# Reordering the passage between the frequency stage and the feed-forward stage of a long-convolution kernel

## The chip, the cores and the metric

The kernel runs on one core of a Trainium2 chip. The metric is the device time of one execution in microseconds (us). A core has a matmul engine (TensorE, PE), a vector engine (VectorE, DVE), a scalar engine (ScalarE, ACT), a general engine (GpSimd, POOL) and a queue engine that only issues transfers (SyncE, SP). Each engine works through its own instructions in order, and waits on semaphores for the others. Matmuls write into PSUM, which has eight banks; DVE and ACT read it, POOL cannot.

## The reference

The reference is a long convolution per channel, done as a product in the frequency domain, followed by a feed-forward layer whose hidden value is the maximum of three products.

```python
h_mlp = np.maximum(pos_emb @ w1, 0.0) @ w2
h_filt = h_mlp * np.exp(-0.01 * pos)[:, None]
u = x * v
Uf = np.fft.rfft(u, n=2 * S, axis=1)
Hf = np.fft.rfft(h_filt, n=2 * S, axis=0)
y = np.fft.irfft(Uf * Hf[None], n=2 * S, axis=1)[:, :S]
t = (x * y).reshape(B * S, D)
h = np.maximum(np.maximum(t @ w1_, t @ w2_), t @ w3_)
out = h @ w_out
```

B is 4, S is 12544, D is 128, and the hidden width is 768. Everything is in 32 bit floating point.

## The kernel before

**Stages.** The Fourier transform is split into factors that are matmuls with tables. For batch 0 a first stage takes 32 units of the product `x*v` to a spectrum `spec`. Then a loop over 46 steps goes through 45 groups of frequencies: second stage (`g_second`), filter spectrum (`s_second`, `s_filter`), product with the filter (`g_re`, `g_im`), and third stage (`g_third`), three steps later than the second. The third stage's result `zs` is copied out of PSUM by ACT and stored to a buffer in memory, `zd`. The feed-forward part then goes over tiles of four positions: it loads z for the tile (`t_load`), makes its even and odd sums (`t_sums`), does the last transform stage and multiplies by x (`t_last`, result `gt`), and then runs six up products (`up`) and six down products (`down`). Batches 1 to 3 are convolved beside the feed-forward part of the batch before them, with steps placed in slots; there `u_products` does the first stage of a unit in three parts: `top` (an ACT copy), `sums` and `fours` (four vector operations each).

**The passage.** Between the loop and the first tile the code does, in this order: unit 0 of batch 1 (`u_first(0)`), the third stage of group 43, unit 1, one fold, the third stage of the last group 44, and the other five folds with two turns between them. A fold multiplies two weight matrices so that the maximum can be done with two differences and a linear term `lin`: it transposes a slice of `w_sb[0]` on PE into a PSUM bank, ACT copies it out (`w1t`), and a later matmul adds into `pl`. `folding` holds the matmul back by two folds. Then the pools of this stage are closed, those of the next are opened in the same memory, and tile 0 and tile 1 are loaded. Units 2, 3 and 4 are done ahead of the first up product.

**Banks.** Third stages, unit 1's first bank and the folds' banks all come from one PSUM pool with three banks under one tag (`cps0`, tag `cv`). A tile takes a bank that has been given back, and a bank is given back when the last instruction that uses its tile is done. The two banks of the folds are used in turn until the last fold. Unit 1's first bank is read last by the first pair of `fours` (L484).

**Queues.** z stores and tables go out on SP, in program order. In the loop `g_third` issues the z store, and the table for a later third stage (`load_dir`) is asked for after it. The z of tile 0 is loaded on POOL's queue, all groups but the last; the last group's two rows go through a small buffer `ze`, stored on SP and ACT and loaded on SP. x for tiles 0 and 1 is loaded on POOL's queue ahead of z. In the feed-forward part an up product uses three PSUM banks in turn (`hps`): the first product is copied out by ACT, the second is taken by DVE in the maximum (L852).

Of the kernel before, what the change touches and what calls it, by code (L numbers as in the profile page):

```python
# [95 lines left out]
def kernel(  # L96
# [15 lines left out]
    nc = tc.nc  # L112
# [4 lines left out]
    NF = DFF // P  # L117
    NK = N1 // 2
# [529 lines left out]
                                    op=op)  # L648
        abs_[g] = ab

    def g_third(g):
        w, ab = ws.pop((g, 1)), abs_.pop(g)
        ps = state["cv"][1].tile([P, 512], FP32, tag="cv", name="ps3")
        for k in range(2):
            for q in range(2):
                halves_mm(ps[:, (2 * k + q) * D:(2 * k + q + 1) * D], w[:, k, q, :],
                          ab[:, k, q, :], k == 0 and q == 0, True)
        if g < NK - 2:
            zs = state["cv"][0].tile([P, 2, 256], FP32, tag="z", name="zs", bufs=2)
        else:  # L660
            zs = lwp.tile([P, 2, 256], FP32, tag="w1", name="zs")
        nc.scalar.copy(zs[:].rearrange("p k f -> p (k f)"), ps[:])
        if g == NK - 1:
            for c in range(2):
                (nc.scalar if c else nc.sync).dma_start(ze[c], zs[64 * c:64 * c + 2])
        nc.sync.dma_start(
            zd[0][2 * g:2 * g + 2].rearrange("k c t f -> (c t) k f"), zs[:])
# [106 lines left out]
    def x_load(b, i, eng):  # L774
        xT = hp.tile([D, 2, 4, NB], FP32, tag="xT", name="xT", bufs=2)
        for c in range(GC):
            eng.dma_start(xT[c * NG:(c + 1) * NG].rearrange("d i p n -> d (i p) n"),  # L777
                          x[:, 4 * i:4 * i + 8, c, b, :])
        xTs[b, i], xTs[b, i + 1] = xT[:, 0], xT[:, 1]

    def t_load(b, i):
        if b == i == 0:
            x_load(b, i, nc.gpsimd)
        zt = hp.tile([N1, 2, 512], FP32, tag="zt", name="zt", bufs=2)
        for c in range(2):
            if b == 0:
                n = NK if i else NK - 1
                (nc.sync if i else nc.gpsimd).dma_start(
                    zt[NK * c:NK * c + n],
                    zd[b].rearrange("(g a) c t f -> g a c t f", a=2)[  # L790
                        0:n, :, c, 2 * i:2 * i + 2, :].rearrange("g a t f -> g a (t f)"))
                if i == 0:
                    nc.sync.dma_start(
                        zt[NK * c + n:NK * c + NK].rearrange("o a (t f) -> o a t f", t=2),
                        ze[c:c + 1].rearrange("o t a f -> o a t f"))
                continue
            q, j = divmod(i, NT // 2)
            for a in range(2):
                nc.sync.dma_start(
                    zt[NK * c:NK * c + NK, a].rearrange("g (t f) -> g t f", t=2),  # L800
                    zd[b].rearrange("(g a) c t q f -> g a c t q f", a=2)[
                        :, a, c ^ (a & q), 2 * j:2 * j + 2, q, :])
        zts[b, i] = zt[:, 0], zt[:, 1]
        if i % 2 == 0 and (b or i > 2):
            x_load(b, i, nc.gpsimd if 0 < i < NT - 2 and b < B - 1 else nc.sync)

# [37 lines left out]
    def up(i, f, tag="hid", bufs=3):  # L844
        rhs = gs[i][:].rearrange("d p n -> d (p n)")
        h = (hidp if tag == "hid" else lp).tile([P, N], FP32, tag=tag, name="hid", bufs=bufs)
        pa = next(hbanks)
        halves_mm(pa[:, 0:N], w_sb[1][:, f * P:(f + 1) * P], rhs, True, True)
        nc.scalar.activation(h[:], pa[:, 0:N], Relu)  # L849
        pb = next(hbanks)  # L850
        halves_mm(pb[:, 0:N], w_sb[2][:, f * P:(f + 1) * P], rhs, True, True)
        nc.vector.tensor_tensor(out=h[:], in0=h[:], in1=pb[:, 0:N], op=ALU.max)  # L852
        return h
# [128 lines left out]
    def load_dir(g, a):  # L982
        w = lwp.tile([P, 2, 2, P], FP32, tag=f"w{a}", name="wt")
        nc.sync.dma_start(w[:].rearrange("p k r m -> p (k r m)"), wt_d[g, :, a, :])
        return w
# [73 lines left out]
    wf, wi = {}, {}  # L1059
# [30 lines left out]
    cps = pro.enter_context(tc.tile_pool(name="cps0", bufs=3, space=PSUM))  # L1090
# [75 lines left out]
    def folding(f):  # L1166
        folded.append(fold(f))
        if len(folded) > 2:
            folded.pop(0)()

    for s in range(NK + 1):
        if s < NK:
            ws[s, 0] = wf[s]
            s_second(s)
            g_second(s)
            wf.pop(s)
            if s + 3 < NK:
                wf[s + 3] = load_dir(s + 3, 0)
        if 1 <= s <= NK:
            g_swap(s - 1)  # L1180
            s_filter(s - 1)
        if s >= 3:
            ws[s - 3, 1] = wi.pop(s - 3)
            g_third(s - 3)
            if s < NK:
                wi[s] = load_dir(s, 1)
        ready = [g for g in {NK: (s - 2, s - 1)}.get(s, (s - 2,)) if 0 <= g and s <= NK]
        for g in {NK - 2: (s - 2, s - 1), NK - 1: (s - 1,), NK: (s - 1,)}.get(s, (s - 2,)):
            if 0 <= g and s <= NK:
                s_store(g)  # L1190
        for g in ready:
            g_re(g)
            g_im(g, 1 < s < NK - 2)
            if s == NK:
                g_unfold(g)
        if s < NK:
            s_sums(s)
            g_butterfly(s)
            for g in ready:
                g_unfold(g)  # L1200

        if s in muls:
            u_mul(muls[s])
        if s in turns:
            u_turn(turns[s])
        if s in loads:
            u_load(1, loads[s])

    def one_bank(pool, tag):
        return pool.tile([P, 512], FP32, tag=tag, name="ps1")[:]  # L1210
# [6 lines left out]
    pl = sps.tile([P, 512], FP32, tag="pl", name="pl")  # L1217
    u_first(1, (one_bank(cps, "cv"), hb), "x")
    fb = one_bank(cps, "cv")
    folds = iter((fb,))  # L1220
    folding(0)
    ws[NK - 1, 1] = wi.pop(NK - 1)
    g_third(NK - 1)
    folds = itertools.cycle((one_bank(cps, "cv"), fb))
    turn_banks = iter((g0, g1))
    state["turn"] = lambda: next(turn_banks)
    for f in range(1, NF):
        folding(f)
        if f in (2, 3):
            u_turn(f + 2)  # L1230
# [17 lines left out]
    cps = conv.enter_context(tc.tile_pool(name="cps", bufs=1, space=PSUM))  # L1248
# [15 lines left out]
    for n, (b, i) in enumerate(tiles[:LAST]):  # L1264
        if i == 0:
            plan, pairs_from = plans[b]
        if n == 0:
            t_load(*tiles[0])
            t_load(*tiles[1])
            nc.gpsimd.dma_start(sign_t[:], sign_d)  # L1270
            second_ = u_products(2, (next(hbanks), next(hbanks)))
            second_[0]()
            first_ = ops.tile([D, 512], FP32, tag="ops", name="ps1")
            spare = state["bank"]()
            third = u_products(3)
            fourth = u_products(4, (spare[:, 0:512], spare[:, 512:1024]), "xs")
            t_sums(tiles[0], nc.vector)
            third[0]()
            second_[1]()
            fourth[0]()  # L1280
            t_last(tiles[0], first_)
            second_[2]()
            for fn in fourth[1:]:
                fn()
        for f in range(NF):

            if i < NT - 2:
                if f == 0:
                    t_load(*tiles[n + 2])
            elif i == NT - 1 and f < 2 and n + 1 + f < len(tiles):  # L1290
                t_load(*tiles[n + 1 + f])
            turn_ = i == NT - 1
            if f == 3 and n == 0:
                x_load(b, 2, nc.gpsimd)
            if f == 4 and n + 1 == LAST:
                t_sums(tiles[n + 2], nc.vector)
            h = up((b, i), f)
            if n == 0 and f in (1, 2):
                third[f]()
            for a in range(2):  # L1300
                if f == plan[i][a]:
                    t_sums(tiles[n + 1],
                           nc.vector if turn_ or i * NF > pairs_from else nc.gpsimd, (a,))
            late.append(((b, i), f, h))
            if len(late) > 2:
                down(*late.pop(0))
            if f == plan[i][2]:
                t_last(tiles[n + 1])
            if f == 5 and n + 1 == LAST:
                t_last(tiles[n + 2])  # L1310
            run(besides.pop(n * NF + f, ()))
# [9 lines left out]
    cps = ctx.enter_context(tc.tile_pool(name="cps2", bufs=1, space=PSUM))  # L1321
# [18 lines left out]
    step, b = 0, B - 1  # L1340
    for i in range(0, NT, 2):
        h = {}
        X, Y = banks if i % 4 == 0 else banks[::-1]
        for j, (name, f) in enumerate(ORDER):
            n = int(name[1]) - 1
# [66 lines left out]
```

## Time and profile before

| what | value |
|---|---|
| median of three runs | 2205.84 us (2205.76 to 2206.69) |
| the profiled execution's own time | 2205.64 us |
| its span, first to last instruction | 2203.9 us |
| PE, DVE, ACT, POOL busy | 2186.5, 1533.7, 1211.4, 1183.3 us |
| frequency loop of batch 0 | about 110 to 268 us |
| passage | about 267 to 288 us |

A share of busy time is an average over stages with different limits. The passage is a hundredth of the span, so it is read in the timeline of the single engines and in stretches of a few us, and not in the page's groups. In the timeline a row gives the start, the duration from the first to the last of merged instructions, engine, line, operation, output and input, the count, and in brackets the idle time ahead of it and what ended it. "SPq" and "ACTq" are rows of a queue that issues transfers.

### The profile page before, as it was taken

The page shows a single profiled execution, that of the slowest core. Times are in us where ns is not written, and L with a number is a line of the kernel's source. Part 1 is how long each engine was busy: PE and PEld are TensorE (multiplying, and loading weights), DVE is VectorE, ACT ScalarE, POOL GpSimd, SP SyncE. Part 2 cuts the span into 40 slices and gives each one's busy share as a digit, 9 for nine tenths or more (in the row PEclk, how much of TensorE's full clock was granted, in tenths as well). Part 3 has the DMA queues.
Part 4 walks back from the last instruction along what each step waited for, and adds up shares of the span by engine and source line. Part 5 has one row for each costly group of instructions (what it writes and reads, how often), then busy time and mean ns, then how long its engine had stood idle before and what let it go on. Part 6 is the DMA issues. An engine that isn't in the chain of part 4 may idle for free.

```text
span 2203.9 us, 77207 instructions
## 1 busy us (share of the span) xinstructions
PE 2186.5 (99%) x31655; PEld 1258.5 (57%) x31655; DVE 1533.7 (70%) x3292; ACT 1211.4 (55%) x2223; POOL 1183.3 (54%) x1580
## 2 busy tenths in 40 slices
PE   9999999999999999999999999999999999999998
PEld 8988855555555555555555455555555545555565
DVE  5688966678888766668888766668878745454443
ACT  3699845466666555466666555456666522222222
POOL 1166568545544667535455566534545326666665
PEclk9999999999999999999999999999999999999999
DMA  8789999879999899789999899879999622222221
GB/s 200 184 262 318 302 181 206 170 196 247 248 245 246 209 189 178 155 193 243 245 245 251 212 193 175 171 172 244 242 251 241 179 75 59 65 71 69 59 59 24
DMA packets 491270, 411.62 MB, mean 187 GB/s; under 512 B 289379, under 2 KB 407901, under 8 KB 490917
## 3 DMA queue, kind: packets, MB, share of 16 engines
q1 hardware_dynamic: 443495, 274.33, 57.5%
q0 software_dynamic: 45936, 130.43, 20.9%
q8 instruction: 249, 4.08, 0.8%
q10 hardware_dynamic: 1486, 1.93, 0.4%
q14 instruction: 104, 0.85, 0.1%
HBM read 262.85 MB, written 84.68 MB: 158 GB/s over the span
## 4 chain that ended last, share of the span: by engine, by line
PE 93%; DVE 2%; POOL 2%; issue 1%; DMA 0%; ACT 0%; POOLq 0%; ACTq 0%; DVEq 0%
PE hps L169 46%; PE ops L169 20%; PE ops L913 6%; PE cps L169 4%; PE cps L549 3%; PE cps L451 3%; PE ps L178 3%; PE cps L559 3%; PE ps L169 2%; POOL xt L640 1%; PE last L169 1%; DVE ab L647 1%; PE ps L393 1%; DVE xs L639 1%; POOL specH L640 1%
## 5 line engine op out<-in xcount | busy, mean ns | idle before, releaser
L169 PE MATMUL hps<-gt,w_sb 128*64 128x392 f32 (+1 forms) x7672 | 1151.8, 494 | 1.8 <-DVE hid L852 1.0
L849 ACT ACTIVATE hid<-hps 128x392 f32<-128x392 f32 x768 | 382.4, 498 | 745.2 <-PE hps L169 726.9
L169 PEld LDWEIGHTS hps<-gt,w_sb 128*64 128x64 f32 (+1 forms) x7672 | 413.7, 126 | 454.5 <-issue 415.9
L852 DVE TENSOR_TENSOR hid<-hid,hps 128x392 f32<-128x392 f32 x768 | 428.5, 558 | 339.9 <-PE hps L169 321.4
L169 PE MATMUL ops<-hid,wo_sb 128*64 128x392 f32 x2304 | 476.8, 492 | 0.0
L601 POOL TENSOR_TENSOR cb<-cb,xs 128x512 f32<-128x512 f32 x135 | 178.2, 1320 | 358.3 <-DVE xs L598 349.8
L169 PEld LDWEIGHTS ops<-hid,wo_sb 128*64 128x64 f32 x2304 | 165.7, 137 | 213.5 <-issue 213.5
L574 DVE TENSOR_TENSOR cb<-cps,eo 128x512 f32<-128x512 f32 (+1 forms) x288 | 175.2, 650 | 78.0 <-ACT eo L571 76.9
L867 POOL DMA_DIRECT2D out_dram<-ot x96 | 77.1, 803 | 263.6 <-ACT ot L865 247.3
L589 ACT ACTIVATE xs<-cb 32x512 f32<-32x512 f32 x270 | 169.5, 628 | 21.9 <-DVE cb L574 13.1
L590 ACT COPY xs<-cb 32x512 f32<-32x512 f32 x270 | 166.3, 616 | 3.1
L605 DVE TENSOR_TENSOR xs<-cb 128x256 f32<-128x256 f32 x270 | 148.3, 598 | 7.3 <-POOL cb L601 7.3
L431 ACT COPY uT<-turned 113x512 uint16<-113x512 uint16 x180 | 125.9, 770 | 1.9 <-DMA turned<-planes 1.7
L388 POOL TENSOR_TENSOR ut<-ut 128x392 f32<-128x392 f32 x90 | 92.8, 1032 | 43.1 <-DMA ut<-in_vr_dram 42.9
L582 POOL DMA_DIRECT2D zd<-cb x135 | 93.8, 695 | 39.9 <-DVE cb L574 36.8
L169 PEld LDWEIGHTS cps<-f4p,even 90*64 90x64 f32 x1552 | 87.2, 138 | 35.9 <-issue 33.1
L777 POOL DMA_DIRECT2D xT<-in_x_dram x172 | 101.4, 605 | 4.6 <-DVE ab L647 3.1
L473 DVE TENSOR_TENSOR low<-high,cps 128x180 f32<-128x180 f32 x186 | 54.7, 336 | 68.9 <-ACT high L463 68.9
L938 POOL DMA_DIRECT2D out_dram<-o x120 | 72.6, 610 | 45.6 <-DVE o L931 44.5
L169 PE MATMUL cps<-f4p,zt 90*64 90x49 f32 x1552 | 95.9, 222 | 0.0
L415 POOL COPY planes<-ut 128x392 uint16<-128x392 uint16 x180 | 94.9, 561 | 0.0
L169 PE MATMUL cps<-f4p,even 90*64 90x49 f32 x1552 | 94.6, 220 | 0.0
(173 smaller groups left out, 3306.1 us busy)
## 6 DMA issues: line engine op xcount, KB each, us to landing
ht<-hd SPq DMA_DIRECT2D x264, 256.0 KB, 6.8
wt<-wq_const POOLq DMA_DIRECT2D x144, 256.0 KB, 5.6
zd<-cb POOLq DMA_DIRECT2D x135, 256.0 KB, 5.1
zt<-zd SPq DMA_DIRECT2D x384, 90.0 KB, 3.8
sq<-spec SPq DMA_DIRECT2D x528, 64.0 KB, 5.9
ut<-in_xr_dram SPq DMA_DIRECT2D x128, 196.0 KB, 4.0
ut<-in_vr_dram SPq DMA_DIRECT2D x128, 196.0 KB, 4.3
wt<-wt_const SPq DMA_DIRECT2D x90, 256.0 KB, 5.1
```

What stands on the lines that cost most here:

```text
L169: nc.tensor.matmul(out[h:h + w], lhsT[:, h:h + w], rhs, start=start, stop=stop, skip_group_check=True)
L415: nc.gpsimd.tensor_copy(w[:, h, :, :, 0:HB], a[:].bitcast(U16).rearrange("p s (m e h) -> p h s e m", e=2, h=2)[:, h])
L431: nc.scalar.copy(uts[u][0:HR, 8 * (u % 2):8 * (u % 2) + 8].rearrange("n s r t -> n (s r t)").bitcast(U16).rearrange("n (s r t h) -> n h s ...
L574: nc.vector.tensor_tensor(out=cb[:, a, lo:hi], in0=ps[:, lo:hi], in1=eo[:, lo:hi], op=op)
L589: nc.scalar.mul(xs[at:at + 32], xt[at + 32:at + 64], -1.0)
L590: nc.scalar.copy(xs[at + 32:at + 64], xt[at:at + 32])
L601: nc.gpsimd.tensor_tensor(out=xts[g], in0=xts[g], in1=xs[:], op=ALU.add)
L605: nc.vector.tensor_tensor(out=ab[:, q], in0=y[:, 0], in1=y[:, 1], op=(ALU.subtract, ALU.add)[q])
L777: eng.dma_start(xT[c * NG:(c + 1) * NG].rearrange("d i p n -> d (i p) n"), x[:, 4 * i:4 * i + 8, c, b, :])
L849: nc.scalar.activation(h[:], pa[:, 0:N], Relu)
L852: nc.vector.tensor_tensor(out=h[:], in0=h[:], in1=pb[:, 0:N], op=ALU.max)
L913: nc.tensor.matmul(ps[32 * q:32 * q + 32, 0:H2], w[:, m:m + 32], rhs[:, H2 * c:H2 * c + H2], start=start, stop=True, skip_group_check=True)
```

## The change

Four edits. (1) Two folds instead of one come ahead of the last third stage, and both banks of the folds are taken there. (2) In the loop the table for a later third stage is asked for inside `g_third`, after its matmuls and ahead of the copy and store of z. (3) The loads of z for tile 0 come ahead of those of x on POOL's queue. (4) Unit 4's `sums` and `fours` come behind the first and the second up product of tile 0, and no longer ahead of the first.

```diff
-    def g_third(g):
+    def g_third(g, then=None):
         w, ab = ws.pop((g, 1)), abs_.pop(g)
         ps = state["cv"][1].tile([P, 512], FP32, tag="cv", name="ps3")
...
                           ab[:, k, q, :], k == 0 and q == 0, True)
+        if then:
+            then()
         if g < NK - 2:
...
     def t_load(b, i):
-        if b == i == 0:
-            x_load(b, i, nc.gpsimd)
         zt = hp.tile([N1, 2, 512], FP32, tag="zt", name="zt", bufs=2)
...
         zts[b, i] = zt[:, 0], zt[:, 1]
+        if b == i == 0:
+            x_load(b, i, nc.gpsimd)
...
-            g_third(s - 3)
-            if s < NK:
-                wi[s] = load_dir(s, 1)
+            g_third(s - 3, (lambda: wi.update({s: load_dir(s, 1)})) if s < NK else None)
...
     fb = one_bank(cps, "cv")
-    folds = iter((fb,))
-    folding(0)
+    folds = itertools.cycle((fb, one_bank(cps, "cv")))
+    for f in range(2):
+        folding(f)
     ws[NK - 1, 1] = wi.pop(NK - 1)
     g_third(NK - 1)
-    folds = itertools.cycle((one_bank(cps, "cv"), fb))
     turn_banks = iter((g0, g1))
     state["turn"] = lambda: next(turn_banks)
-    for f in range(1, NF):
+    for f in range(2, NF):
         folding(f)
...
             t_last(tiles[0], first_)
             second_[2]()
-            for fn in fourth[1:]:
-                fn()
         for f in range(NF):
...
             h = up((b, i), f)
+            if n == 0 and f < 2:
+                fourth[f + 1]()
             if n == 0 and f in (1, 2):
                 third[f]()
```

## The prediction

> **What bounds the kernel now.** I read the page first: TensorE is busy for 2186.5 of 2203.9 us. So only places where PE stands idle, or where the change adds PE work, can matter, and the change adds no instruction. Next I cut the span into stretches of 2 us around the passage from the frequency stage to the feed-forward stage (the columns are PE, PEld, DVE, ACT and POOL busy time with counts, granted clock, DMA share, GB/s).
>
> ```profile
> core 0: us, PE busy (x) PEld busy (x) DVE busy (x) ACT busy (x) POOL busy (x), PEclk, DMA share, GB/s
> ...
> 270.00:272.00 2.00, 1.00 (x36) 0.73 (x29) 1.86 (x5) 1.06 (x3) 0.00 (x0) 1.00 0.88 294
> ...
> 282.00:284.00 2.00, 1.10 (x30) 0.98 (x32) 1.89 (x7) 0.00 (x0) 0.15 (x1) 1.00 0.09 28
> ...
> 286.00:288.00 2.00, 0.97 (x8) 0.29 (x6) 1.97 (x7) 0.50 (x1) 0.47 (x1) 1.00 0.94 254
> ```
>
> PE lacks 1.00, 0.90 and 1.03 us here, and the DVE column is nearly full: VectorE is the busy engine. From 262 to 288 us these stretches lack 6.0 us of PE in all; from 288 on every stretch is full. The change is spent inside a pool of about 6 us. The chain of waits (start, duration, what) tells what the end hangs on there.
>
> ```profile
> 268.59 1.24 PE ps L169 x16
> ...
> 270.46 4.16 DMA zd<-zs
> ...
> 275.23 0.67 POOL zt L788
> 275.90 4.79 DMA zt<-zd
> ...
> 280.76 0.70 DVE even L818
> ...
> 283.30 0.57 DVE gt L839
> ...
> 287.28 0.48 DVE hid L852
> ```
>
> Stage three of group 43, its z store, the reload of z for tile 0, the even and odd sums, `gt`, then the first up products at 283.92 us. While z travels, PE has folds, turns and products of units 2 to 4 until 281.06, so it waits for the reload by only 0.50 and 0.35 us. The timeline of single engines gives the rest.
>
> ```profile
> 271.85 1.09 PE L169 MATMUL ps<-ab,wt 128*64 128x128 f32 x16 [1.00 <-DMA wt<-wt_const]
> ...
> 273.62 0.44 PE L1099 MATMUL ps<-eye,w_sb 128*128 128x128 f32 x2 [0.68 <-ACT zs L662]
> ...
> 275.21 0.59 DVE L484 TENSOR_TENSOR spec<-ps,low 128x180 f32<-128x180 f32 x2
> ...
> 275.88 1.46 SPq L793 DMA_DIRECT2D zt<-ze  x2
> ```
>
> The first line is the last third stage (group 44). The next is two fold transposes, which waited for that stage's copy out of PSUM: the second fold bank is taken after the last third stage and is that stage's own bank. The DVE line is the first pair of sums in `fours` of unit 1; it ends at 275.80 and is the last that reads unit 1's first bank.
>
> **Part 1, two folds ahead.** The pool `cps0` has three banks. Today: third stage 43 in one, unit 1 in the next, `fb` in the third, and the last third stage back in the first, which the copy at 269.85 empties by 270.43. After the change the second fold bank is taken before the last third stage. Both fold banks are held until the last fold, so unit 1's bank is the only one left for that stage. It comes free when DVE has done unit 1's `fours`. DVE works in order and with no gap over 0.1 us from 267.3 to 276.3 (xt, xs, ab of 44, unit 0, unit 1), and nothing upstream of it is touched, so 275.80 stands. The last third stage moves from 271.85 to 275.85: **4.0 us late**, and PE, in order, stands from about 271.2 (the first transpose starts at 270.52, and two take 0.33 each) for 4.6 us. Were the other bank given to the fold instead, its transpose would wait for the same DVE line ahead of the stage: the same 4.0.
>
> What follows on PE: today it is 8.12 us from 272.94 to the end of unit 4's products at 281.06, of which 0.98 are waits (0.68 for the copy, 0.30 for `w1t`). Afterwards the 0.68 goes (fold 2 has a bank of its own), one transpose of 0.26 is already done, and the `w1t` copies still come behind the `uT` copies on ACT (0.3 to 0.5). So 276.94 + 7.14 - 0.26 + 0.4 = 284.2, **3.15 us later** than today.
>
> The end of z for group 44 goes through `ze`: copy ends at 277.56, store issued 277.60; today the store went out at 273.59 and the load that waits for its landing at 275.88, so 2.3 us: loads at 279.9 and 280.65. Their landing isn't shown. Lower bound 2.3 (like their store), upper 4.9 (the reload on POOL, 45 times as large); I take 2.3, since both are 4 KB. `even` starts at 283.0, and from `even` to the up products it is 3.16 today (280.76 to 283.92): 286.2. By PE: 284.2 + 0.95 for tile 0's products + 0.65 for `gt` = 285.8. So the up products start near 286.2, **+2.3**.
>
> **The clock.** No gap of 4.6 us stands in today's trace between matmuls, but its two ends bear on it (PE busy, count, granted clock, DMA share, GB/s).
>
> ```profile
> 4.00:5.00 1.00, 1.00 (x8) 1.00 0.88 234
> ...
> 11.00:12.00 1.00, 1.00 (x14) 1.00 1.05 288
> ...
> 2200.00:2201.00 1.00, 0.00 (x0) 0.80 0.76 160
> 2201.00:2202.00 1.00, 0.00 (x0) 0.50 0.03 7
> ```
>
> The last matmul ends at 2198.04; the clock is halved at about 2200.6, that is 2.6 us later. In the first us the same matmul runs 8 times per us, later 12 to 14, and the switch comes some 4.7 us after the first matmul. A gap of 4.6 us is well above 2.6, so I expect PE to come back at half clock: each us of that loses 1 - 8/13 = 0.38. Bounds: nothing (the drop misses) and 4.7 x 0.38 = 1.8; I take 1.1, about 3 us at half clock. The products of unit 4 then end at 285.3, tile 0's at 286.25, `gt` at 286.9, up products at 286.95: **+3.0**. The Trainium skill (TensorE: Matmul & The Clock Gate, "What's actually happening" and "Why this matters for your kernels") has a free-running window of about 3.4 us, halves the clock after one idle window, and warns of gaps over some 3 us. By a wholly idle window, a 4.6 us gap would be caught only in (4.6 - 3.4)/3.4, an estimated third of phases, and the sum would more often be the +2.3; the drop 2.6 us after the last matmul says that a partly busy window is enough.
>
> **Part 2, tables ahead of z stores.** Same issues (0.42 and 0.37 us each on SP), swapped 42 times. The table's buffer is free when the third stage ends (202.05 in one step), 0.6 to 1.3 us before the z copy ends (203.28), so the store isn't held. PE waits for a table only once, the 1.00 above, and there `ab` of 44 (DVE, 270.91 to 271.67) comes within 0.15 of it: worth 0.15 alone, nothing behind part 1. In the loop no PE wait for tables is listed between 120 and 262 us: 0. Against it: a z store that shares the queue with an earlier table. It lands 4.9 after 203.31, at 208.2, and its buffer is rewritten at 209.53: 1.3 us of cover. Beyond that each tenth would cost up to 4.2 us over 42 steps; 0.4 (one issue) leaves it hidden. I take 0.
>
> **Part 3, z ahead of x on POOL's queue.** Six issues instead of four then two: x took 2.35 us (4 x 0.59), from 272.41 to 274.76, while POOL could only wait for the z store, which landed at 274.62. So z gains 0.1 (up to 0.5 if x's transfers no longer slow it), hidden behind the `ze` trip. x now leaves at 276 to 278.5 and lands by about 282.2 (3.7 in this stretch), before `gt` needs it: 0. Uncovered it would cost what it passes 286. Behind x on POOL there is only the sign vector and, 5 us on, tile 1's sums, which wait for SP's reload anyway.
>
> **Part 4, unit 4's sums behind up products.** Today DVE does unit 4's 8 sums between `gt` and the first maximum (287.20), and the third up product waits 1.03 for that bank. Afterwards the first maximum comes when its products end, 1.5 us after the up products start, and frees the bank at 2.05, before PE wants it at 2.9. The sums then fill DVE up to unit 3's last pair at 7.7, before tile 1's products need that bank at 8.5. **-1.03**; between 0 (if the next join on ACT, which at 299.93 already waits 0.27 for its transposed planes, holds PE back) and -1.03.
>
> **Sum**: +3.0 - 1.0 = +2.0. The profiled execution took 2205.64 us (span 2203.9 and 1.74 around it), 0.2 below the median of the runs, so **2207.6**.
>
> **Rivals.** (A) is the forecast, 0.50. (B) the bank wait without the half clock: +2.3 - 1.0 = +1.3, 2206.9; for it, the drop at the end of the trace followed a gap with no end: 0.18. (C) the trip of the last pair takes over as the bound: with a landing of 4.9, `even` starts at 285.6, the up products at 288.75, +4.8 - 1.0 = +3.8; with its store as slow as the other z stores (4.2 instead of 2.3) +5.7; about 2210.4. It decides once the landing passes 284; for it, the DMA queues carry z, x and f4p at once; against it, today's 2.3 with the same neighbours: 0.22. (D) not slower: the last third stage gets a bank without waiting, because the folds let go of one earlier than I read. Then 0.15 of part 2, some 0.15 of part 3 and part 4's 1.0 remain: 2204.3; against it, three banks and both folds' use up to the end: 0.10. That a part does nothing (2 and 3 here) is in all four.
>
> **Numbers.** A difference under 0.2% (4.4 us) is about what a measurement of this kernel can't tell from none. Above +4.4 lie some 0.6 of C and 0.08 of A: 0.17. Below -4.4 nothing is worked out; 0.02 for what I overlooked. Same: 0.81. A's own range is +0.9 to +3.8 (clock 0 to 1.8, part 4 kept or half lost). The range takes in D's edge and most of C: 2204.0 to 2210.8.
>
> **What would show it.** Right: the last third stage at about 275.8, released by DVE's spec sums; a PE hole of over 4 us before it; granted clock below 1.00 after it; up products near 287; no PE wait for the maximum after the second up product. Wrong: a last third stage near 271.8 (D), or clock at 1.00 (B), or `even` later than 284 (C); and any ACT wait ahead of the z copies in the loop would break part 2's zero.

## The result and the profile after

The changed kernel takes **2209.49 us** at the median (2207.91 to 2212.54), the kernel before, run beside it, 2206.83 us (2205.28 to 2209.60). The ratio is 1.0013 with an interval of 1.0007 to 1.0018: 2.7 us more, inside the 0.2% that the prediction called no difference, though the interval does not reach 1. The profiled execution took 2209.07 us with a span of 2207.3 us, 3.4 more than the one of before; 0.6 of that lies ahead of the passage, for unit 0 of batch 1 starts at 268.25 us, before at 267.66.

The stretches of 2 us come first again. The columns are PE, PEld, DVE, ACT and POOL busy time with counts, granted clock, DMA share, GB/s.

```profile
core 0: us, PE busy (x) PEld busy (x) DVE busy (x) ACT busy (x) POOL busy (x), PEclk, DMA share, GB/s
272.00:274.00 2.00, 0.00 (x0) 0.00 (x0) 1.97 (x7) 0.05 (x1) 0.00 (x0) 1.00 0.52 178
274.00:276.00 2.00, 0.00 (x0) 0.00 (x0) 2.00 (x9) 0.00 (x0) 1.18 (x2) 0.64 0.00 0
...
278.00:280.00 2.00, 2.00 (x18) 1.45 (x17) 0.00 (x0) 0.85 (x2) 1.07 (x2) 0.50 0.89 183
280.00:282.00 2.00, 2.00 (x23) 1.47 (x21) 0.00 (x0) 0.75 (x2) 0.00 (x0) 0.65 0.62 183
282.00:284.00 2.00, 2.00 (x26) 1.22 (x21) 0.00 (x0) 1.82 (x4) 0.00 (x0) 1.00 0.02 8
...
290.00:292.00 2.00, 2.00 (x15) 0.86 (x12) 1.48 (x5) 0.71 (x2) 0.49 (x1) 1.00 0.73 204
```

Where PE lacked 1.00 us of a stretch before, two whole stretches are now empty while DVE is full. The granted clock then falls to 0.50, and a full PE does 18 instructions in 2 us there against 26 at clock 1.00. The last stretch is full; before, the one with the wait for the maximum (286 to 288 us) lacked 1.03.

The chain of waits (start, duration, what):

```profile
272.06 4.42 issue
276.48 1.97 PE ps L169 x16
...
287.06 1.09 PE ps L169 x32
...
288.17 0.58 DVE gt L841
...
288.79 4.17 PE hps L169 x24
```

Before, the chain went along z: the store of group 43, its reload, `even`, `gt`. Now none of these is in it. PE's hole, the last third stage, PE's own filler and `gt` follow each other. The 24 matmuls of the first three up products run through in 4.17 us; before, they were 16 and 8 with the wait between, 5.42 us in all:

```profile
283.92 2.85 PE L169 MATMUL hps<-gt,w_sb 128*64 128x392 f32 x16 [0.67 <-DVE gt L839]
287.80 1.54 PE L169 MATMUL hps<-gt,w_sb 128*64 128x392 f32 x8 [1.03 <-DVE hid L852]
```

The timeline of single engines:

```profile
276.48 1.97 PE L169 MATMUL ps<-ab,wt 128*64 128x128 f32 x16 [4.94 <-issue]
...
275.79 0.59 DVE L484 TENSOR_TENSOR spec<-ps,low 128x180 f32<-128x180 f32 x2
...
281.95 1.47 SPq L793 DMA_DIRECT2D zt<-ze  x2
...
284.78 0.69 DVE L820 TENSOR_TENSOR even<-zt 90x512 f32<-90x512 f32 x1 [7.90 <-DMA zt<-ze]
```

The last third stage starts 0.10 us after the DVE row of unit 1's sums ends (275.79 + 0.59 = 276.38), after a hole of 4.94 us. The row itself names no releaser ("issue"), so here this rests on the times; the first experiment has a row that names it. Its 16 matmuls take 1.97 us against 1.09 before. `even` starts at 284.78, while PE's filler runs until 286.99 (the first of tile 0's products), so the trip of z through `ze` isn't what the up products wait for.

### The profile page after: what moved, and what is told of

Same layout as the page of the kernel before. It is cut to its first block, busy times and chain, and to the rows that moved or that the text cites. A ratio compares the mean times of both kernels' runs of the same rounds, so it can differ in the third digit from the quotient of the medians.

```text
span 2207.3 us, 77202 instructions
## 1 busy us (share of the span) xinstructions
PE 2187.9 (99%) x31655; PEld 1293.1 (59%) x31655; DVE 1533.6 (69%) x3292; ACT 1211.3 (55%) x2223; POOL 1185.8 (54%) x1580
## 4 chain that ended last, share of the span: by engine, by line
PE 93%; POOL 2%; DVE 2%; issue 2%; ACT 1%; DMA 0%; POOLq 0%; ACTq 0%; DVEq 0%
PE hps L169 46%; PE ops L169 20%; PE ops L915 6%; PE cps L169 4%; PE cps L549 3%; PE cps L451 3%; PE ps L178 3%; PE cps L559 3%; PE ps L169 1%; POOL xt L640 1%; PE last L169 1%; DVE ab L647 1%; PE ps L393 1%; DVE xs L639 1%; POOL specH L640 1%
## 5 line engine op out<-in xcount | busy, mean ns | idle before, releaser
L169 PEld LDWEIGHTS hps<-gt,w_sb 128*64 128x64 f32 (+1 forms) x7672 | 431.2, 126 | 438.2 <-issue 383.4
```

What stands on the lines that cost most here:

```text
L169: nc.tensor.matmul(out[h:h + w], lhsT[:, h:h + w], rhs, start=start, stop=stop, skip_group_check=True)
```

## The experiments

Each kernel is compared with the kernel before, run beside it. Where the text gives a place in the passage, it is taken from PE's start of unit 0 of batch 1, since the loop ahead of it ends anywhere from 267.7 to 270.2 us whatever the kernel. "PE short" in the tables is PE's idle time from 255 to 296 us in gaps of over 0.08 us, worked out from the matmul records; the times at half clock are those of the trace's clock records.

### Does the second fold bank make the hole?

`p1_alone` is the kernel before with edit (1) alone; `no_p1` is the changed kernel without it.

```diff
-    folds = iter((fb,))
-    folding(0)
+    folds = itertools.cycle((fb, one_bank(cps, "cv")))
+    for f in range(2):
+        folding(f)
     ws[NK - 1, 1] = wi.pop(NK - 1)
     g_third(NK - 1)
-    folds = itertools.cycle((one_bank(cps, "cv"), fb))
...
-    for f in range(1, NF):
+    for f in range(2, NF):
```

> Part 1 alone. Theory (the last third stage waits for unit 1's bank, and PE comes back at half clock): last third stage 4.0 to 4.6 us later than before's 271.85, granted clock at 0.50 after the hole, up products some 4.3 later, and the 1.03 us wait for the maximum still there, so +3 to +4.5 us in all: slower than the whole change. Rival (the loss comes from tables ahead of z stores): no change, within 0.5 us.

> Parts 2, 3 and 4 without part 1. Theory: last third stage near 271.8, clock at 1.00 throughout, the wait of 1.03 us gone: -1.0 to -1.5 us against before. Rival (tables ahead of z stores cost the 0.6 us by which the changed kernel was late ahead of the passage, or more): 0 to +1 us, with the steps before the passage later than before's.

| kernel | median, us | before beside it | ratio (95%) | last third stage | hole ahead of it | up products |
|---|---|---|---|---|---|---|
| p1_alone | 2211.89 | 2207.86 | 1.0018 (1.0009 to 1.0026) | 8.24 | 4.94 | 19.74 |
| no_p1 | 2206.88 | 2207.86 | 0.9993 (0.9984 to 1.0001) | 3.77 | 0.58 | 15.82 |
| the changed kernel | 2209.49 | 2206.83 | 1.0013 (1.0007 to 1.0018) | 8.24 | 4.94 | 20.54 |
| before | | | | 4.19 | 1.00 | 16.26 |

PE rows of `p1_alone`, then of `no_p1`:

```profile
278.41 1.98 PE L169 MATMUL ps<-ab,wt 128*64 128x128 f32 x16 [4.94 <-DVE spec L484]
...
293.79 1.54 PE L169 MATMUL hps<-gt,w_sb 128*64 128x392 f32 x8 [1.02 <-DVE hid L852]
```

```profile
272.94 1.17 PE L169 MATMUL ps<-ab,wt 128*64 128x128 f32 x16 [0.58 <-ACT w1t L1103]
```

With edit (1) alone the profile names the releaser outright: the `spec` sums at L484, the last readers of unit 1's bank. Without the edit the hole is gone. The loss belongs to edit (1), 4.0 us by itself (2.0 to 5.7 by its interval). `no_p1` was expected to keep its clock and to gain 1.0 to 1.5 us; its clock fell to one half at 284.8 us, and its interval does not exclude no change.

The changed kernel itself was run once more beside other kernels:

> The changed kernel once more, for a second execution's trace. Theory: the hole ahead of the last third stage is 4.9 us again, released by unit 1's sums; the clock falls to 0.50 again, for one or two windows of 3.4 us by where the hole lies in them; +2 to +4 us against before. Rival (the half clock was chance): clock at 1.00, last third stage to first up product 11 us and not 12.3.

`after2`: 2210.63 us against 2207.45, ratio 1.0009 (1.0000 to 1.0018). The last third stage stands at 8.23, the hole is 4.93 us, the up products come at 20.2: the passage repeats to 0.4 us.

### Is it the memory bank, or being two folds ahead?

`halves4` keeps two folds ahead, but in two halves of the one fold bank, so that the other bank stays with the last third stage. It has edit (4) too.

```diff
-    folds = iter((fb,))
-    folding(0)
+    folds = itertools.cycle((fb, fb[:, 2 * D:]))
+    for f in range(2):
+        folding(f)
...
-    folds = itertools.cycle((one_bank(cps, "cv"), fb))
```

> Two folds ahead, but into the two halves of one bank, so that the last third stage keeps a bank of its own; and part 4. Theory (the bank is the whole harm of part 1): last third stage within 0.3 us of where it is with part 4 alone, no wait of 0.68 us for its copy behind it, no half clock; time -1.0 to -1.8 against before. Rival (two folds ahead are late for another reason): last third stage over 2 us later, slower than before.

Measured: 2206.23 us against 2207.91, ratio 0.9988 (0.9977 to 0.9999). PE rows:

```profile
272.65 0.33 PE L1099 MATMUL ps<-eye,w_sb 128*128 128x128 f32 x1 [0.50 <-ACT w1t L1101]
272.91 1.09 PE L169 MATMUL ps<-ab,wt 128*64 128x128 f32 x16
```

Two transposes ahead of the third stage, and no wait in front of it: it stands at 3.94, with edit (4) alone at 3.96. The bank makes the hole, and not being two folds ahead. The order of the folds isn't quite free (the up products stand at 16.65, with edit (4) alone at 16.10), and the clock, which was expected to hold, fell at 286.2 us.

### What does the clock cost?

`warm` is the changed kernel with 16 pairs of products of no use (64 matmuls) ahead of the last third stage, written to columns of `pl` that nothing reads. They fill the hole but for 1.30 us, and leave the bank wait. `p1_warm` is the same on edit (1) alone.

```diff
+    for _ in range(16):
+        halves_mm(pl[:, 2 * D:3 * D], wo_sb[:, 0, :], wo_sb[:, 0, :], True, True)
     ws[NK - 1, 1] = wi.pop(NK - 1)
     g_third(NK - 1)
```

> The changed kernel with 16 pairs of matmuls of no use (4.3 us at full clock) ahead of the last third stage, in the hole. Theory: clock stays at 1.00, the last third stage starts where it did (released by unit 1's sums), and from there to the up products it takes about 10.4 us and not 12.3: 1 to 2 us less than the changed kernel, +0.5 to +1.5 against before. Rival (the z trip sets the up products, the clock costs nothing): same time as the changed kernel, up products 12.3 after the last third stage.

> Part 1 alone with the same 16 pairs of matmuls of no use in the hole, part 4 left out. Theory (half clock costs 1 to 2 us in the passage; the kernel with the pairs and part 4 gave that back at the joins of 310 to 340 us, because PE had run ahead of the transposed planes): without part 4 PE is 1.03 us less ahead, so the holes from 296 us on sum to under 1.0 us (2.5 with part 4), and the time is 0.5 to 2 us below part 1 alone. Rival (the pairs themselves cost something, or half clock costs nothing in the end): at or above part 1 alone.

`warm`: 2211.20 us against 2207.86, ratio 1.0015 (1.0007 to 1.0024). `p1_warm`: 2211.55 against 2207.91, ratio 1.0016 (1.0003 to 1.0028). PE rows of `warm`:

```profile
272.59 3.71 PE L169 MATMUL pl<-wo_sb 128*64 128x128 f32 x64
277.60 1.09 PE L169 MATMUL ps<-ab,wt 128*64 128x128 f32 x16 [1.30 <-issue]
...
286.18 0.32 PE L169 MATMUL ps<-f4p,even 90*64 90x49 f32 x4 [0.22 <-issue]
...
288.55 3.84 PE L169 MATMUL hps<-gt,w_sb 128*64 128x392 f32 x22 [0.67 <-DVE gt L841]
```

The clock is kept: the third stage is back at 1.09 us. From its start to the end of the units' products PE takes 8.36 us, in the changed kernel 10.57, so the half clock costs 2.2 us of PE. But only 1.36 of that reaches the up products (10.95 against 12.31 after the third stage), for now the trip of z binds: tile 0's products wait 0.22 for `even`. And the total is no better: +3.3 us against the kernel before, where +0.5 to +1.5 was expected. The waits from 290 to 345 us show why (engine, line, releaser: total, times, longest), first of the changed kernel, then of `warm`:

```profile
ACT uT L431 <- DMA turned<-planes: 0.9, 1, 0.9
```

```profile
ACT uT L431 <- DMA turned<-planes: 9.9, 5, 2.9
...
PE hps L169 <- ACT hid L851: 1.6, 3, 0.8
```

The turned planes of later units come through POOL and a transposing transfer on SP's queue. In `warm` they come late, ACT stands in front of them, its copies of the up products come late, and PE gaps by 1.9 us more than in the changed kernel from 296 us on (2.55 against 0.62).

That this comes of PE being early was the idea behind `p1_warm`, where PE is 1.03 us less ahead; its gaps from 296 us on were expected under 1.0 us, its time 0.5 to 2 us below `p1_alone`. The first did not come, and the second isn't seen:

```profile
ACT uT L431 <- DMA turned<-planes: 8.6, 5, 3.5
```

The gaps are 4.05 us, and its ratio isn't told from that of `p1_alone` (the profiled execution, 2215.92 us, lies 4.4 above its median). In `warm` the loads of the later units start as far behind the first up product as in the changed kernel (1.09 and 1.10 us), so PE isn't ahead of them; the third transposing transfer takes 4.71 us on its queue there and 2.51 in the changed kernel. So an early PE is not shown to be the cause of the late planes.

`warm_ut` is `warm` with the loads of units 6, 7 and 8 asked for earlier on SP's queue, right behind tile 1's load.

```diff
             t_load(*tiles[1])
+            for u in (6, 7, 8):
+                u_load(1, u)
...
-            at(load_, 0, u_load, b, u)
+            if b > 1 or load_:
+                at(load_, 0, u_load, b, u)
```

> The changed kernel with the pairs in the hole, and with the loads of units 6 to 8 asked for right behind tile 1's z, ahead of tile 2's. Theory (PE ran ahead of the transposed planes): the loads go out some 3 to 5 us earlier against the up products, ACT's waits for turned planes between 290 and 345 us fall from 9.9 to under 3, the PE holes from 296 us on from 2.5 to under 1.0, and the time is 1 to 2 us below that of the kernel with the pairs. Rival (the transposes are slow of themselves, wherever their input comes): holes as before, same time.

Measured: 2209.19 us against 2207.91, ratio 1.0008 (0.9996 to 1.0019). ACT no longer waits for turned planes from 290 to 345 us, and PE's gaps from 296 us on are 0.59. So the late planes are what held ACT, and earlier loads take the wait away. From unit 0 of batch 1 to the end this profile is 1937.6 us long, those of the changed kernel 1939.0 and 1938.7, that of `warm` 1940.5; the time can't be told from that of the changed kernel, nor surely from `warm`'s.

### The other parts, one at a time

`p4_alone`, `p2_alone` and `p3_alone` are the kernel before with that edit alone, as in the diff of the change. `before2` is the kernel before, profiled again.

```diff
-            for fn in fourth[1:]:
-                fn()
...
             h = up((b, i), f)
+            if n == 0 and f < 2:
+                fourth[f + 1]()
```

> Part 4 alone. Theory: the PE wait for the first maximum (1.03) is gone and nothing else moves: -1.0 us, from -1.03 to -0.5. Rival (the next join on ACT takes the wait over): 0, with PE holes of together 1 us between 290 and 310.

> Part 2 alone. Theory: no effect in the loop; the wait for the last table ahead of the last third stage (0.8 to 1.0 us) shrinks to the wait for ab (0.6): 0 to -0.3 us, not told from none. Rival (z stores and filter stores land later behind earlier tables and hold ACT): ACT waits for stores in the loop that before doesn't have, PE holes ahead of 262 us larger by over 0.5 us, +0.6 us or more.

> Part 3 alone. Theory: z of tile 0 on POOL is still released by the z store of group 43, tile 0's sums still by the last group's load on SP; x is there in time: no change, within 1 us. Rival (x was in z's way): even some 0.5 us earlier against the last third stage than 8.9.

> The kernel before once more, one look. Theory: its holes between 281 and 288 us (together some 2.5) are at the edge for the clock, which fell there in three of the five executions seen without the long hole; here it may or may not. Ahead of the passage ACT waits for stores in the loop by 0.2 to 2 us as it comes, so the passage begins up to 2 us later than in the first profile, with no change made. Rival (those waits come from part 2): under 0.5 us of such waits here.

| kernel | median, us | before beside it | ratio (95%) |
|---|---|---|---|
| p4_alone | 2205.80 | 2207.86 | 0.9990 (0.9981 to 0.9998) |
| p2_alone | 2208.51 | 2207.91 | 0.9999 (0.9988 to 1.0011) |
| p3_alone | 2207.56 | 2207.45 | 0.9999 (0.9990 to 1.0008) |

PE rows, and a wait from 290 to 345 us, of `p4_alone`:

```profile
285.42 4.17 PE L169 MATMUL hps<-gt,w_sb 128*64 128x392 f32 x24 [0.67 <-DVE gt L839]
```

```profile
PE hps L169 <- ACT hid L849: 0.7, 1, 0.7
```

The wait of 1.03 us is gone, as in the changed kernel, and 0.72 of it comes back at 306.9 us, where ACT's copy of an up product is late behind turned planes. Even so edit (4) is the one part that gains beyond its interval.

Waits of ACT in the loop (112 to 262 us) of `p2_alone`:

```profile
ACT ht L1153 <- DMA hd<-ht: 2.2, 3, 1.2
...
ACT zs L664 <- DMA zd<-zs: 0.4, 1, 0.4
```

The second line is what the prediction said would break its zero for edit (2): ACT waits for a z store before it can refill the buffer. It stands in five of the seven profiles of kernels with the edit and in one of the seven without it. The cover of 1.3 us is used up now and then, but the loop is no longer for it: unit 0 starts at 268.96 us on average with the edit and at 269.17 without. In the passage this profile is later than those of before: PE waits 1.60 us for `even`, the clock is at half for 6.8 us, and the up products stand at 17.5 where 16.3 and 16.4 were; `no_p1`, which has the edit too, has them at 15.8, and the medians of `p2_alone` show no loss.

In `p3_alone` `even` stands 8.7 us behind the last third stage, in the two profiles of before 8.9 and 9.4, which doesn't tell whether x was in z's way.

`before2` (2207.19 us, span 2205.4) shows what the first profile of before didn't. Its passage begins 1.4 us later, as was expected, but not for the expected reason: ACT waits for no store between 112 and 262 us. PE in stretches of 1 us (busy, clock, DMA share, GB/s):

```profile
core 0: us, PE busy (x), PEclk, DMA share, GB/s
282.00:283.00 1.00, 0.00 (x0) 1.00 0.63 186
...
285.00:286.00 1.00, 0.61 (x2) 0.50 0.01 2
...
287.00:288.00 1.00, 1.00 (x4) 0.50 0.72 177
288.00:289.00 1.00, 1.00 (x8) 0.92 0.99 265
```

The kernel before loses the clock here too, from 284.7 to 288.2 us, just as its up products begin: 4 in a us instead of 8.

```profile
285.39 5.52 PE L169 MATMUL hps<-gt,w_sb 128*64 128x392 f32 x24 [0.67 <-DVE gt L839]
```

These 24 take 5.52 us without a wait for the maximum, where the first profile took 5.42 with it: slower products give DVE the time that PE waited before. In `p3_alone` the clock falls earlier:

```profile
274.00:276.00 2.00, 1.32 (x15) 0.90 (x11) 2.00 (x9) 0.85 (x2) 0.00 (x0) 0.79 0.20 69
276.00:278.00 2.00, 2.00 (x17) 1.46 (x13) 1.50 (x6) 0.52 (x2) 1.56 (x3) 0.50 0.69 188
```

| kernel | PE short 255 to 296 us | clock at half, us | us at half |
|---|---|---|---|
| before | 5.87 | none | 0 |
| before2 | 5.51 | 284.7 to 288.2 | 3.4 |
| p3_alone | 5.34 | 275.2 to 278.6 | 3.4 |
| p4_alone | 5.66 | none | 0 |
| no_p1 | 4.68 | 284.8 to 288.2 | 3.4 |
| halves4 | 5.20 | 286.2 to 289.6 | 3.4 |
| p2_alone | 6.59 | 285.2 to 292.1 | 6.8 |
| the changed kernel | 7.72 | 274.6 to 281.4 | 6.8 |
| after2 | 7.37 | 273.9 to 280.7 | 6.8 |
| p1_alone | 8.47 | 278.1 to 281.5 | 3.4 |
| best (below) | 6.43 | 284.7 to 291.5 | 6.8 |
| warm | 4.58, and 3.7 of no use | none | 0 |
| p1_warm | 5.18, and 3.7 of no use | none | 0 |
| warm_ut | 4.45, and 3.7 of no use | none | 0 |

### A version meant to beat both

`best` is `no_p1` with the early loads of `warm_ut`.

> Parts 2, 3 and 4 without part 1, and the loads of units 6 to 8 asked for behind tile 1's z, ahead of tile 2's. Theory: part 4's 1.0 us is kept in every execution, since the joins have some 3 us more slack: -1.0 to -2.0 us against before, below each kernel so far. Rival (the joins took nothing back on average): as parts 2, 3 and 4 alone, -0.7 to -1.5.

It missed: 2208.55 us against 2207.45, ratio 1.0006 (0.9997 to 1.0015). The DVE row ahead of the up products:

```profile
284.84 0.57 DVE L842 TENSOR_TENSOR gt<-ps,xT 128x392 f32<-128x392 f32 x1 [1.33 <-DMA xT<-in_x_dram]
```

x comes behind z by edit (3), and the three early loads now travel beside it. It lands at 284.72 us, 5.3 to 6.7 after its issue (4.5 to 4.8 in `no_p1`), `gt` waits 1.33 us for it and PE 1.89. The cover that made edit (3) free is gone once other loads travel beside it. The clock then stays at half for 6.8 us, in `no_p1` for 3.4. The quickest kernels are `p4_alone` (0.9990) and `halves4` (0.9988), which their intervals do not tell apart; both are quicker than the kernel before, by some 2 us of the 2208, and than the changed one by more.

## Why the prediction was right, and where its terms were off

**The forecast case held.** The last third stage waits for unit 1's bank, released by the `spec` sums, with a hole of over 4 us, a clock below 1.00 behind it and no wait for the maximum. Of the five signs that the prediction named these four are there; the fifth, up products near 287 us, isn't: they came at 288.79, or 288.2 without the 0.6 us by which the loop ended later. One sign named for rival C, `even` later than 284, is there too (284.78), but PE's filler ran longer still, so C did not bind.

**Bank wait.** Predicted 4.0 us, measured 4.05 (8.24 against 4.19 after unit 0). The hole was put at 4.6 us and measured 4.94. PE's filler behind it, without the clock, was worked out at 8.35 us and measured at 8.36 in `warm`.

**The clock was mis-sized.** The prediction took 1.1 us, from about 3 us at half clock. It is 6.8 us in both profiles of the changed kernel, of which 4.9 and 4.1 lie behind the hole, and it costs 2.2 us of PE in the first. The same hole in `p1_alone` is followed by 3.4 us at half clock, and the filler takes 9.76 us there, 1.4 more than in `warm`; that would have fitted the term. In the changed kernel the filler takes 10.57 us where 9.45 was forecast; that 1.12 is nearly all by which the up products came later than worked out (+4.28 against +3.0; the rest is 0.05 of the bank wait and 0.1 in tile 0's products and `gt`). By the third up product 1.25 us are saved (4.17 against 5.42), which leaves 3.0; from unit 0 to the end the two first profiles differ by 2.8 us (1939.0 against 1936.2), and the medians by 2.7, where +2.0 was forecast.

**The range of the forecast case doesn't come out of its terms.** They give +1.3 (z's trip, no half clock, edit (4) kept) to +3.2 (1.8 for the clock, half of edit (4) lost), and not +0.9 to +3.8. And of the 1.9 us between the forecast of 2207.6 us and the 2209.49 measured, 1.2 lie in the kernel before, which took 2206.83 us beside the changed one and 2205.64 in the execution from which the sum starts.

**The kernel before was read from an execution that kept its clock.** The prediction charged the half clock to the changed kernel alone, while in six of the eight profiles of kernels without the long hole the clock falls somewhere in the passage as well. In the kernel before this costs little, since it falls where PE would have waited for the maximum: from unit 0 to the end `before2` is 0.2 us longer than the first profile. The mean granted clock of each run, on record to three places, leans the same way (3.4 us at half clock take 0.0008 of it): of 97 runs of the kernel before, 21 have 1.000 and 60 have 0.999, with mean times of 2207.8 and 2207.6 us. So reading one execution did not mislead the sum by more than that.

**The trip of z.** The issue at 279.11 us and the load's row at 281.95 are 2.84 us apart, where 2.3 was taken; the second load lands 1.9 us after its issue, where 2.3 was taken too. The rival in which this trip binds was priced with a landing of 4.9 and didn't come about: the loads landed sooner, and half clock made PE's filler longer. Of the kernels with edit (1), `even` holds PE only in `warm` and `warm_ut`, with the clock kept, by 0.22 and 0.29 us.

**No half clock.** That rival is excluded for the changed kernel by two profiles, and by the mean granted clock, which is 0.998 or less in 31 of its 33 runs and in 16 of 97 of the kernel before. `warm` is that rival in kind, and it is not faster: in its trace the 1.36 us saved by the up products are given back at the later joins.

**Edit (4).** The 1.03 us are gained at the place named. The lower bound, that a join on ACT takes it back, is visible in part: 0.72 in `p4_alone`, none in the changed kernel, where ACT waits 0.9 us for turned planes against 4.6; why they come sooner there is not shown. Where the clock falls on these products the gain is not there: the 24 take 5.75 us in `no_p1`, with the edit, and 5.52 in `before2`, without. By time the edit is worth 2.1 us (0.4 to 4.2 by its interval), which holds the 1.03.

**Edits (2) and (3).** Zero fits both (0.9999 each, known to some 2.5 us). For edit (2) the cover was thinner than worked out, though no time is seen to come of it; for edit (3) `best` shows what was said of lost cover, 1.3 us of wait.

**What stays open.** Which executions lose the clock, and when, wasn't settled: the idle time just ahead doesn't decide it alone (below). That the join waits cost `warm` what the kept clock gave is read from one trace, and its share of the time is within the interval; why the transposing transfers are slow in some executions is open.

## What to carry to other kernels

When a loop takes its PSUM tiles from a pool, moving one allocation ahead of another hands the second a different bank: work out whose bank that is, and who reads it last, before the order of the instructions is judged. Two halves of a bank may do where a second bank was taken. And before a half clock is charged to a change, look in more than one profile of the kernel before whether it falls there already, and what it costs there.

## What the runs showed of the hardware that was not expected

The granted clock fell to one half behind stretches in which PE was only partly idle: 1.24 us idle in the 3.41 us ahead of it in `no_p1`, 1.38 in `before2`, 1.75 in `p3_alone`. It held after 1.03 in the kernel before, after 1.30 in `warm`, and in `before2` after one gap of 1.64 us that ended at 266.95 us, so this amount alone doesn't decide. Each half-clock interval in the passage lasted 3.41 or 6.83 us, one or two of the same length. In each of the 14 traces all changes of the clock after the first lie a whole number of such lengths behind the first: in the changed kernel 269.65 us, 79 lengths, from the rise at 4.91 us to the fall at 274.56. So where a gap lies against this grid may be what tells executions apart; no run tests it. The Trainium skill (TensorE: Matmul & The Clock Gate, "What's actually happening") has the clock halved after at least one idle window of some 3.4 us; the length agrees, but here no window had to be wholly idle.

The third transposing transfer of the feed-forward part, of one size in all kernels, took from 1.5 to 5.0 us on its queue (4.4 before, 2.5 after, 4.7 in `warm`, 5.0 in `p4_alone`, 1.5 in `p2_alone`). Long ones often go with long waits of ACT for turned planes (9.9 us in `warm`, 4.6 in `p4_alone`, none in `p2_alone`), but not always: in `halves4` it took 4.0 us, and ACT did not wait. And a reload of 4 KB through `ze` landed 1.9 us after its issue in the changed kernel, but 4.6 to 4.7 in `no_p1` and `p4_alone`, where z and the other loads were still on the way.
